# An earlier weight fold, another norm check and a new instruction order in a fused attention and gMLP kernel

## The chip, the cores and the metric

The kernel runs on one core of a Trainium2 chip. The metric is the device time of one execution in microseconds (us). The kernel before takes 265.9 us as the median of three runs (265.62 to 266.1).

An execution's profile has a span that is some 2 us shorter than its time. Stages below are read from the profiles. A ratio is the mean time of one kernel's fast runs over that of the other's in the same rounds, so it is not quite the ratio of the medians that are quoted.

## The reference

Two residual blocks over one sequence of 2,048 tokens with 448 features, both modulated by a condition vector `c`. The first is linear attention with 16 heads of 28 features and the feature map (softmax(p), softmax(-p)). The second is a gated MLP with a 2,048 by 2,048 spatial product.

```python
mod = (silu(c) @ w_mod).reshape(1, 6, 1, -1)          # sa, ca, ga, sb, cb, gb
h = layernorm(x) * (1 + ca) + sa
q, k, v = split_heads(h @ wqkv)
pq, pk = q @ w_phi, k @ w_phi                         # per head, 28 x 28
phi_q = concat(softmax(pq), softmax(-pq));  phi_k = concat(softmax(pk), softmax(-pk))
o = (phi_q @ (phi_k.T @ v)) / (phi_q @ sum(phi_k) + 1e-6)
x = x + ga * (o @ wo)
h = layernorm(x) * (1 + cb) + sb
z = gelu(h @ w_in);  z1, z2 = halves(z)
g = w_sp @ layernorm(z2) + b_sp                       # over tokens
x = x + gb * ((z1 * g) @ w_out)
```

## The kernel before

All weights that meet `h` are prepared on the chip. The per-head matrix `w_phi` is folded into the key weight (fold: transpose of the weight, `fold_T`, then a product with a block-diagonal copy of `w_phi`, called `BD`, `fold_pf`), its rows are scaled by 1 + ca, and the shift sa becomes one more row. The start-up in program order:

```python
    nc.scalar.dma_start(out=x_sb[:, 0:2, :], in_=xv[:, 0:2, :])             # x first on the ACT ring
    load_rows(nc.sync, wk_raw[:, :, 0:D], A_wqkv[:, D:2 * D])               # key weight, two loads
    nc.scalar.dma_start(out=wm1[:, :, D:960], in_=wmod_v[:, :, D:960])      # scale columns
    nc.sync.dma_start(out=phi[:], ...)                                      # w_phi
    nc.sync.dma_start(out=wm1[:, :, 0:D], in_=wmod_v[:, :, 0:D])            # shift columns
    # ... (cut)
    l1_rstd(0)                                                              # GpSimd
    l1_apply(0, nc.vector)
    nc.gpsimd.tensor_tensor(out=BD[:]..., in0=phi[:]..., in1=bmask[:]..., op=ALU.mult)
    # ... (cut)
    fold_T(wk_raw, wTk, False)
    cf = colform((1,))                                                      # 1 + ca as columns
    # ... (cut)
    own_turn(0)                                                             # first tile's transposes
    cf = colform((0,))                                                      # sa as columns
    # ... (cut)
    fold_sa(wk_raw, wTk)
    # ... (cut)
    for m in range(3):
        fold_pf(wTk, Wk, m, m % 2)
    fold_pf(wTk, Wk, 3, 1)
```

Everything behind the start-up is one long table of words. Each word is a step, and the order of the words is the program order on every engine; nothing else reorders them.

```python
    steps = dict(k=k_, e=e_, v=v_, ..., wsp=load_wsp, num=num_, t=t_, ad=ad_, oT=oT_, wo=wo_, h2T=hT_, z2=z2_, z1=z1_, zg=zg_, ...)
    for word in ORDER.split():
        name, *args = word.split(".")
        # ... (cut)
        steps[name](*map(int, args))
```

The words that the argument needs: `k`, `e`, `v`, `kv` are a tile's key product, exponentials, value product and key-value product, `kb1` copies their sum (the tile KVbd). Then `num` is the attention product of a tile, `t` its scaling on VectorE, `ad` an addition on GpSimd, `oT` a transpose by DMA, `wo` the output product (tile x_ps). `h2T` is the DMA transpose of the next normalised tile, `z2` and `z1` the two halves of the input product (both z_ps), `zg` the gelu of a z1 bank (it writes z1T). `wsp` loads and transposes a piece of the spatial weight, on the same queue as `oT` and `h2T`:

```python
    def load_wsp(tcn, u):
        q, hf = divmod(u, 2)
        r0 = tcn * TCHF + q * P
        nc.sync.dma_start_transpose(out=wsp_tiles[tcn][:, hf * 8:(hf + 1) * 8, q * P:(q + 1) * P],
                                    in_=B_w_sp[r0:r0 + P, hf * 1024:(hf + 1) * 1024])
    def oT_(i):
        oTs[i] = sm2.tile([P, KC, P], BF, name="oT", tag="oT", bufs=4)
        nc.sync.dma_start_transpose(out=oTs[i][:], in_=opad[i % NO][:])
    def zg_(st, fc):
        nc.scalar.activation(out=z1T[:, fc, st * 512:(st + 1) * 512], in_=ps.pop(("z1", st, fc)), func=ACT.Gelu_apprx_tanh, bias=b1[:, fc:fc + 1])
```

A check decides whether the fast path was allowed: a bound on the norm of the folded weights, made of 16 products (`gr`) and a square (`grc`). If it fails, a general path runs, which it doesn't for these inputs.

Of the kernel before, what the change touches and what calls it, by code (L numbers as in the profile page):

```python
# [8 lines left out]
ACT = mybir.ActivationFunctionType  # L9
# [6 lines left out]
P = 128  # L16
# [464 lines left out]
BY_ACT = (14, 15)  # L481
# [8 lines left out]
cc wv.1 k.0 bn.3 wv.0 wv.3 bv ag.3 wv.2 e.0.0 rp.1 bn.5 ld.7 k.1 bn.4 bvc ld.8 e.0.1 ag.5 ag.4 bn.6 gr.0 rp.2 e.1.1 ld1.2 rd.0 e.1.0 fq.1 grc.0 tm.2  # L490
v.1 to.2 fqc.3 la1.5 ld1.3 fqc.1 fq.0 bn.8 la1.4 vc.1 k.2 rc.0 fqc.0 bn.7 lT.4 tm.3 fqc.2 ag.8 v.0 e.2.0 to.3 ag.7 ag.6 v.2 mu.0 lT.5 rp.3 vc.0 rd.1
e.2.1 pq.1 v.3 vc.2 ld.3 bn.9 pqc.1 sq la1.7 rc.1 kv.0 vc.3 bn.10 pq.0 sqc la1.6 k.3 bn.11 pqc.0 ag.10 mu.1 lT.6 k.4 e.3.0 ag.9 rd.2 e.3.1 gt.0 rp.4
e.4.1 lT.7 pq.3 rd.3 e.4.0 k.5 pqc.3 ld.4 v.4 ca rc.2 gtc.0 ag.11 mu.2 e.5.0 v.5 e.5.1 wg.1 rc.3 vc.4 kv.1 rd.4 la1.9 pq.2 kv.2 vc.5 la1.8 lT.9 mu.3
k.6 pqc.2 rp.5 bn.12 sa.15 v.6 bn.13 lT.8 k.7 rd.5 vc.6 la1.10 v.7 e.6.0 ag.12 ag.13 rc.4 rp.6 e.7.1 rc.5 qp.0 lT.10 e.6.1 e.7.0 rd.6 sa.14 la1.11 q.4
mu.4 la1.12 lT.11 rd.7 cfb qe.4.0 la1.13 kv.3 rc.6 lT.12 cfc rp.7 k.8 qe.4.1 mu.6 vc.7 mu.5 k.10 e.8.1 ld.9 rc.7 kv.4 mu.7 la1.14 e.10.1 k.9 e.10.0
la1.15 lT.14 v.8 rd.10 e.9.1 e.8.0 kv.5 lT.13 e.9.0 k.11 rd.8 v.11 e.11.1 lT.15 rd.9 e.11.0 v.9 vc.8 rc.8 wsp.0.7 kv.6 qpe.0.1 rc.9 mu.8 k.12 rc.10
vc.9 kv.7 rd.11 ld.6 e.12.0 v.10 e.12.1 mu.9 vc.11 kv.8 ld.5 rc.11 vc.10 k.14 mu.10 k.13 rd.12 e.14.0 kv.9 mu.11 e.13.1 v.12 e.13.0 rc.12 kv.10 rd.13
vc.12 v.13 qpe.0.0 k.15 mu.12 e.14.1 rc.13 kv.11 vc.13 rd.14 v.14 e.15.0 kv.12 mu.13 vc.14 qp.1 rc.14 e.15.1 rd.15 kv.13 mu.14 v.15 rc.15 mu.15 kv.14
vc.15 wb.3 wg.0 qpe.1.1 wg.3 kv.15 zb qpe.1.0 kb1 wb.2 zbc kb2 wg.2 num.0 ws.0 num.1 sx.0 q.7 ws.3 sx.1 wbc.2 cr.0 q.6 cr.1 dn.0 dn.1 qe.7.0 ri.0 ri.1
w.0 w.1 wbc.3 q.5 t.0 qe.7.1 t.1 qe.5.1 ad.0 num.2 q.8 qe.6.0 ws.2 sx.2 ad.1 qe.6.1 oT.0 num.3 cr.2 ws.1 q.9 sx.3 qe.8.1 dn.2 oT.1 cr.3 ri.2 q.14 dn.3  # L500
qe.8.0 w.2 ri.3 t.2 qe.5.0 q.11 qe.14.1 w.3 ad.2 t.3 num.4 wo.0 sx.4 qe.14.0 oT.2 cr.4 ad.3 num.6 dn.4 qe.9.1 xc.0 q.15 qe.11.1 ri.4 ls.0 oT.3 qe.11.0
wo.1 w.4 la.0 t.4 qe.15.1 rs.0 q.13 sx.6 qe.15.0 xc.1 num.5 qe.9.0 cr.6 ap.0 q.10 ls.1 sx.5 qe.13.1 dn.6 ad.4 cr.5 la.1 h2T.0 q.12 dn.5 ri.6 ri.5
qe.10.1 w.5 w.6 rs.1 t.5 qe.10.0 wo.3 oT.4 qe.12.0 t.6 qe.12.1 num.8 ap.1 wo.2 sx.8 xc.3 qe.13.0 ad.5 h2T.1 z2.0 cr.8 xc.2 tb ad.6 dn.8 ls.2 oT.5 ri.8
gr.1 la.2 w.8 ls.3 ge.0 rs.2 oT.6 t.8 wo.4 num.7 ap.2 zs.0.0 z2.1 sx.7 la.3 zs.0.1 h2T.2 cr.7 za.0 dn.7 rs.3 ri.7 wo.5 w.7 wsp.0.1 ge.1 t.7 num.10
zs.1.0 ap.3 z2.2 xc.4 sx.10 ad.8 h2T.3 cr.10 zs.1.1 dn.10 ls.4 ad.7 wo.6 oT.8 ge.2 ri.10 la.4 w.10 za.1 t.10 rs.4 grc.1 num.9 oT.7 z1.0.4 xc.5 sx.9
xc.6 z2.3 ap.4 ls.5 cr.9 h2T.4 zs.2.0 ad.10 dn.9 z1.0.0 zs.2.1 ge.3 ri.9 wsp.0.2 la.5 w.9 wo.7 za.2 t.9 zn.0 rs.5 z2.4 oT.10 zs.3.0 zg.0.4 ls.6 ad.9
zs.3.1 num.12 wsp.0.0 ge.4 wo.8 xc.7 ap.5 za.3 la.6 sx.12 z1.0.5 ls.7 zn.1 rs.6 oT.9 cr.12 zs.4.0 num.11 zg.0.0 la.7 dn.12 z1.0.6 zs.4.1 h2T.5 sx.11
zg.0.5 ri.12 ap.6 cr.11 z1.0.3 w.12 zn.3 za.4 t.12 rs.7 h2T.6 wo.9 zn.2 dn.11 xc.8 z2.5 wsp.0.6 ri.11 xc.9 ap.7 w.11 ls.8 h2T.7 wo.10 t.11 ge.5 z1.0.2
zg.0.6 ad.11 zs.5.0 num.14 zs.5.1 z2.6 ad.12 oT.11 sx.14 cr.14 la.8 dn.14 za.5 ri.14 rs.8 w.14 xc.10 z1.0.1 ge.6 t.14 z1.1.3 zg.0.2 ap.8 zs.6.0 zg.0.3
num.13 ls.9 ad.14 z2.7 h2T.8 sx.13 zs.6.1 zn.4 cr.13 la.9 dn.13 za.6 oT.12 ri.13 wo.11 rs.9 w.13 ge.7 t.13 z1.1.0 zg.1.3 ls.10 num.15 ap.9 zs.7.0  # L510
zg.1.0 z2.8 la.10 ad.13 sx.15 zs.7.1 h2T.9 zn.6 za.7 xc.11 rs.10 wo.12 oT.13 ge.8 ls.11 z1.1.6 zg.0.1 oT.14 zs.8.0 ap.10 zn.5 z1.1.4 la.11 cr.15
zs.8.1 z2.9 h2T.10 dn.15 zg.1.6 za.8 ri.15 xc.12 rs.11 ls.12 wsp.0.3 z1.1.2 w.15 ge.9 t.15 ap.11 wo.14 zg.1.2 zs.9.0 h2T.11 ad.15 z1.1.5 zn.8 zs.9.1
wo.13 za.9 zn.7 oT.15 la.12 rs.12 z2.10 xc.13 xc.14 ap.12 ls.14 z1.1.1 ge.10 ls.13 z2.11 h2T.12 zg.1.1 zs.10.0 zg.1.4 la.13 zs.10.1 z1.2.1 za.10 ge.11
# [7 lines left out]
def fast_path(tc, A_x, A_wqkv, A_w_phi, A_wo, B_w_in, B_w_sp, B_b_sp, B_w_out, c, w_mod, out, flag):  # L521
# [781 lines left out]
```

## Time and profile before

| | kernel before |
|---|---|
| time, median of 3 | 265.9 us |
| span of the profile | 263.7 us |
| mean granted TensorE clock | 0.989 |
| first key product (k_ps) | 11.82 us |
| first exponential sum on VectorE | 15.39 us |
| key-value copy | 54.06 us |
| first spatial product (g_ps) | 139.40 us |

The page and the stages are read in the prediction below. Two more views matter for what came of it. The first is the timeline of TensorE between key-value copy and spatial product: start, duration, engine, line, operation, tiles written and read, shapes, count, and in brackets the idle time before it and what ended it.

```profile
86.01 0.93 PE L1087 MATMUL x_ps<-f_wo,oT 128*128 128x448 bf16 x4 [0.56 <-DVE w L1048]
...
93.31 0.93 PE L1087 MATMUL x_ps<-f_wo,oT 128*128 128x448 bf16 x4 [0.65 <-DMA oT<-f_opad]
...
120.03 1.69 PE L822 MATMUL z_ps<-f_win,h2T 128*128 128x448 bf16 x8 [0.31 <-DMA h2T<-f_xpad]
```

TensorE idles here for transposes that come late. (At 86.01 us the profile names a VectorE step, but the weight load of the same products had waited 1.06 us for oT.) The second view is the timeline of the SyncE queue that issues these transposes, with GpSimd's addition that makes the last tile, just ahead of the wait at 93.31 us.

```profile
85.46 1.31 SPq L996 DMA_TRANSPOSE f_wsp<-in_B_w_sp_dram  x1
87.31 1.19 SPq L1066 DMA_TRANSPOSE oT<-f_opad  x1
88.54 1.30 SPq L996 DMA_TRANSPOSE f_wsp<-in_B_w_sp_dram  x1
88.80 1.03 POOL L1062 TENSOR_TENSOR f_opad<-t 128x448 bf16<-128x448 bf16 x1
89.96 1.20 SPq L1066 DMA_TRANSPOSE oT<-f_opad  x1
```

Each transpose holds the queue for 1.2 to 1.3 us, one after the other. The token transpose at 89.96 us, for which TensorE waits at 93.31, stands directly behind a piece of the spatial weight (88.54 + 1.30 = 89.84) that is not needed before 139 us. In the queue that piece cost it next to nothing, though: GpSimd finished the tile only at 89.83 us. What came late was the landing, 3.31 us after the issue, where the median of these transposes is 2.5 us.

### The profile page before, as it was taken

Reading aid. Unit: us, or ns where it says so; the run is one execution under the profiler, and the core shown is the slowest. Engines: PE = TensorE matmul, PEld = TensorE weight load, DVE = VectorE, ACT = ScalarE, POOL = GpSimd, SP = SyncE. Lnnn points to the kernel's source line nnn. Section 1 sums busy time; section 2 is a strip of 40 time slices with the busy share of each in tenths; the row PEclk is TensorE's granted clock in tenths of the full one; section 3 lists DMA queues with packets and bytes.
Section 4 is the critical chain, followed back from the end, with each engine's and each line's share of the span. In section 5 each row is a group of like instructions: output and inputs, shape, how many; then the busy total and the mean of one; then the engine's idle time right before and its main releaser. Section 6 shows DMA issues by size and latency. Waiting matters only on the chain.

```text
span 263.7 us, 4389 instructions
## 1 busy us (share of the span) xinstructions
PE 250.0 (95%) x1564; PEld 129.6 (49%) x1584; DVE 163.7 (62%) x360; ACT 107.8 (41%) x212; POOL 90.3 (34%) x200
## 2 busy tenths in 40 slices
PE   6899999999999999999998999999999999999991
PEld 3766566665564545444443444444444444444440
DVE  4799999899999989875142454352433443342540
ACT  2799978578854758778895000000000000000000
POOL 5678970006776878757140190000000000000000
PEclk9799999999999999999999999999999999999998
DMA  7957976602456853442399999901000000001002
GB/s 196 307 151 142 199 108 118 223 0 42 80 85 105 125 110 62 87 94 40 66 212 184 243 157 207 194 18 37 17 0 17 20 20 15 0 20 35 19 20 62
DMA packets 69057, 25.29 MB, mean 96 GB/s; under 512 B 59105, under 2 KB 68898, under 8 KB 69026
## 3 DMA queue, kind: packets, MB, share of 16 engines
q1 hardware_dynamic: 68146, 24.18, 45.0%
q10 hardware_dynamic: 880, 0.75, 1.0%
q8 instruction: 14, 0.23, 0.4%
q14 instruction: 17, 0.14, 0.2%
HBM read 8.92 MB, written 1.84 MB: 41 GB/s over the span
## 4 chain that ended last, share of the span: by engine, by line
PE 73%; DVE 11%; DMA 6%; issue 3%; POOL 2%; ACT 1%; SPq 1%; DVEq 0%; POOLq 0%; ACTq 0%
PE g_ps L1195 37%; PE z_ps L822 8%; PE o_ps L1202 8%; PE k_ps L822 5%; PE v_ps L822 5%; DVE t L1056 4%; DMA h2T<-f_xpad 3%; PE kvacc L856 3%; DMA f_wm<-in_w_mod_dram 2%; DVE z2st L1110 2%; PE q_ps L822 2%; PE x_ps L1087 2%; DVE f_x L1091 1%; DMA oT<-f_opad 1%; POOL rs L1121 1%
## 5 line engine op out<-in xcount | busy, mean ns | idle before, releaser
L1195 PE MATMUL g_ps<-f_wsp,f_z2n 128*128 128x512 bf16 x327 | 73.7, 379 | 1.3 <-ACT f_z1T L1160 0.8
L1195 PEld LDWEIGHTS <-f_z2n 128*128 128x128 bf16 x448 | 43.8, 98 | 52.9 <-issue 1.1
L1197 DVE TENSOR_TENSOR gb<-g_ps,f_bsp 128x512 f32<-128x512 f32 x28 | 19.4, 692 | 67.9 <-PE g_ps L1195 67.9
L1247 ACT CAST ot<-o_ps 128x224 bf16<-128x224 f32 x1 | 0.3, 346 | 115.8 <-PE o_ps L1202 115.8
L822 PE MATMUL z_ps<-f_win,h2T 128*128 128x448 bf16 (+1 forms) x128 | 27.0, 352 | 0.5 <-DMA h2T<-f_xpad 0.5
L822 PE MATMUL z_ps<-h2T,f_win 128*128 128x512 bf16 (+1 forms) x107 | 26.6, 379 | 0.4
L1110 DVE BATCH_NORM_STATS2 z2st<-z2g 128x6 f32<-128x448 bf16 x32 | 19.2, 615 | 12.4 <-ACT z2g L1149 12.4
L1062 POOL TENSOR_TENSOR f_opad<-t 128x448 bf16<-128x448 bf16 x16 | 16.7, 1057 | 26.4 <-DVE t L1056 24.4
L1195 PE MATMUL g_ps<-f_hT,f_z2n 128*128 128x512 bf16 x110 | 24.9, 379 | 0.1
L1202 PE MATMUL o_ps<-f_wout,f_z1T 128*128 128x448 bf16 x112 | 23.5, 352 | 0.0
L1198 DVE TENSOR_TENSOR f_z1T<-gb,f_z1T 128x512 bf16<-128x512 f32 x28 | 20.7, 740 | 1.5 <-DVE gb L1197 0.5
L1149 ACT ACTIVATE z2g<-z_ps 128x896 bf16<-128x896 f32 x16 | 14.7, 919 | 14.5 <-PE z_ps L822 13.3
L1160 ACT ACTIVATE f_z1T<-z_ps,f_b 128x512 bf16<-128x512 f32 x28 | 18.2, 686 | 0.4 <-PE z_ps L822 0.4
L822 PEld LDWEIGHTS <-h2T 128*128 128x128 bf16 (+1 forms) x128 | 12.0, 97 | 12.2 <-DMA h2T<-f_xpad 1.3
L840 DVE TENSOR_REDUCE ksum<-f_E 128x32 f32<-128x896 bf16 x16 | 17.0, 1072 | 1.5 <-ACT f_E L829 1.4
L1153 ACT ACTIVATE f_z2n<-z2g,nm,rs 128x896 bf16<-128x896 bf16 x16 | 17.7, 1131 | 0.4 <-POOL nm L1124 0.3
L1056 DVE TENSOR_TENSOR t<-num,w 128x896 bf16<-128x896 f32 x16 | 17.2, 1087 | 0.4
L822 PEld LDWEIGHTS <-f_win 128*128 128x128 bf16 x112 | 10.7, 97 | 12.5 <-DMA h2T<-f_xpad 0.5
L829 ACT ACTIVATE f_E<-k_ps 128x448 bf16<-128x448 f32 x32 | 15.9, 549 | 1.8 <-PE k_ps L822 1.6
L1202 PEld LDWEIGHTS <-f_z1T 128*128 128x128 bf16 x112 | 11.0, 98 | 10.9
L822 PEld LDWEIGHTS <-f_hT 128*128 128x128 bf16 (+1 forms) x128 | 11.8, 98 | 8.8 <-issue 0.2
L1087 PE MATMUL x_ps<-f_wo,oT 128*128 128x448 bf16 x64 | 14.7, 352 | 1.2 <-DMA oT<-f_opad 0.6
(149 smaller groups left out, 340.2 us busy)
## 6 DMA issues: line engine op xcount, KB each, us to landing
out_dram<-ot SPq DMA_DIRECT2D x15, 112.0 KB, 1.7
f_x<-in_A_x_dram SPq DMA_DIRECT2D x3, 448.0 KB, 6.5
f_win<-in_B_w_in_dram SPq DMA_DIRECT2D x2, 672.0 KB, 7.2
f_wm<-in_w_mod_dram SPq DMA_DIRECT2D x1, 840.0 KB, 5.5
f_wout<-in_B_w_out_dram SPq DMA_DIRECT2D x1, 784.0 KB, 5.6
f_bsp<-in_B_b_sp_dram SPq DMA_DIRECT2D x1, 512.0 KB, 4.8
f_wm<-in_w_mod_dram ACTq DMA_DIRECT2D x1, 448.0 KB, 5.4
f_wm<-in_w_mod_dram SPq DMA_DIRECT2D x1, 392.0 KB, 5.5
```

What stands on the lines that cost most here:

```text
L822: nc.tensor.matmul(out, lhsT=lhs(kc, last[kc]), rhs=rhs(kc, last[kc]), start=(kc == 0), stop=(kc == KC - 1))
L840: nc.vector.tensor_reduce(out=cs["s", i][:], in_=Ering[i % NR][:].rearrange("p s (c f h) -> p (s c) h f", c=4, h=HP), axis=AX.X, op=ALU.add)
L1056: nc.vector.tensor_tensor(out=ts[i][:, 0:2 * D].rearrange("p (s h d) -> p s h d", s=2, h=H), in0=nv(i)[:, :, :, 0:DH], in1=cs.pop(("w", i) ...
L1062: nc.gpsimd.tensor_tensor(out=opad[i % NO][:, 0:D], in0=t[:, 0:D], in1=t[:, D:2 * D], op=ALU.add)
L1087: nc.tensor.matmul(ps["x", i][:, 0:D], lhsT=oT[:, cc, :], rhs=wo_s[:, cc, :], start=(i in RES_DVE and cc == 0), stop=(cc == KC - 1))
L1110: nc.vector.bn_stats(out=cs["z", i][:, hf, :], in_=z2gs[i][:, hf * D:(hf + 1) * D])
L1153: nc.scalar.activation(out=z2n[:, i, :], in_=z2gs.pop(i)[:], func=ACT.Identity, scale=rstd[:, 1:2], bias=nmr[:, 1:2])
L1160: nc.scalar.activation(out=z1T[:, fc, st * 512:(st + 1) * 512], in_=ps.pop(("z1", st, fc)), func=ACT.Gelu_apprx_tanh, bias=b1[:, fc:fc + 1])
L1195: nc.tensor.matmul(g[:], lhsT=z2n[:, s_, fc * P:(fc + 1) * P], rhs=wsp_tiles[tcn][:, s_, :], start=(s_ == 0), stop=(s_ == NT - 1))
L1197: nc.vector.tensor_tensor(out=gb[:], in0=g[:], in1=bsp[:, tsl], op=ALU.add)
L1198: nc.vector.tensor_tensor(out=z1T[:, fc, tsl], in0=gb[:], in1=z1T[:, fc, tsl], op=ALU.mult)
L1202: nc.tensor.matmul(o_ps, lhsT=z1T[:, fc, t * P:(t + 1) * P], rhs=wout_s[:, fc, :], start=(first and fc == 0), stop=(fc == FC - 1))
```

## The change

Its intent: fold the key weight before the shift is known, so that only the shift row is left when the shift columns land; start the scale columns and w_phi earlier; make the norm check cheaper on TensorE; move two tiles' statistics from ScalarE to VectorE; and lay a new order table over all of it. The diff, cut to its core:

```diff
-BY_ACT = (14, 15)
+BY_ACT = ()
 ORDER = """            (all words rearranged; two excerpts of the last lines)
-... z1.3.2 za.15 rs.18 zn.13 zg.3.3 zn.15 zg.3.0 zg.3.2 zg.3.4
+... zs.14.1 zg.3.4 ... zs.15.1 zg.3.3 zn.14 z1.3.0 za.15 rs.18 zg.3.2 zn.13 zn.15 zg.3.5 zg.3.0
 # loads
+    nc.scalar.dma_start(out=wk_raw[0:64, 3, 0:D], in_=A_wqkv[3 * P:D, D:2 * D])
+    nc.sync.dma_start(out=wk_raw[:, 0:3, 0:D], in_=A_wqkv[0:3 * P, D:2 * D]...)
     nc.scalar.dma_start(out=x_sb[:, 0:2, :], in_=xv[:, 0:2, :])
-    load_rows(nc.sync, wk_raw[:, :, 0:D], A_wqkv[:, D:2 * D])
     nc.scalar.dma_start(out=wm1[:, :, D:960], in_=wmod_v[:, :, D:960])
 # start-up
-    l1_rstd(0)
-    l1_apply(0, nc.vector)
     nc.gpsimd.tensor_tensor(out=BD[:]..., in0=phi[:]..., in1=bmask[:]..., op=ALU.mult)
+    l1_rstd(0)
     ...
+    l1_apply(0, nc.vector)
+    l1_apply(1, nc.vector)
+    keep_busy(2)
+    columns(cf_c, wmc, 128)                  # with fillers of 128 columns
     ...
+    turn_mm(0)
+    for m in range(3):
+        fold_pf(wTk, m)                      # unscaled, ahead of the shift
     ...
+    columns(cf_s, wms, 128)
     ...
+    fold_sa(wk_raw, sa_ps)
+    fold_pf(wTk, 3)
-    keep_busy(2, 256)
 # norm check
+    def gs_(which):
+        nc.scalar.activation(out=Wsq[:, 0:3, 0:D], in_=W[:, 0:3, 0:D], func=ACT.Square)
+        nc.scalar.activation(out=Wsq[0:65, 3, 0:D], in_=W[0:65, 3, 0:D], func=ACT.Square)
     def gr_(which):
-                nc.tensor.matmul(ps["gr", which][:, cc * CB:(cc + 1) * CB], lhsT=W[...], rhs=W[0:KB[kk], kk, cc * CB:(cc + 1) * CB], ...)
+                nc.tensor.matmul(ps["gr", which][:, cc:cc + 1], lhsT=Wsq[...], rhs=ones[0:KB[kk], :], ...)
```

## The prediction

> **What bounds the kernel now.** I read the page first: the granted clock is near full, TensorE is busy 95% of the span, and part 4 gives the chain that ended last 73% of TensorE.
>
> ```profile
> PE 250.0 (95%) x1564; PEld 129.6 (49%) x1584; DVE 163.7 (62%) x360; ACT 107.8 (41%) x212; POOL 90.3 (34%) x200
> ...
> PE 73%; DVE 11%; DMA 6%; issue 3%; POOL 2%; ACT 1%; SPq 1%; DVEq 0%; POOLq 0%; ACTq 0%
> ```
>
> So I looked for the 13.7 us in which TensorE is not busy, with the table of stretches (columns: stretch, length, then busy us and count for PE, PEld, DVE, ACT, POOL, then clock, DMA share, GB/s).
>
> ```profile
> 8.40:12.00 3.60, 3.56 (x56) 3.29 (x57) 2.54 (x6) 2.41 (x6) 2.90 (x20) 0.54 1.11 323
> 12.00:20.00 8.00, 8.00 (x75) 5.15 (x73) 8.00 (x23) 7.51 (x18) 5.40 (x12) 0.99 0.66 177
> 20.00:30.00 10.00, 10.00 (x94) 6.20 (x93) 10.00 (x20) 9.19 (x22) 8.52 (x17) 1.00 0.78 163
> ...
> 74.00:84.00 10.00, 9.46 (x77) 5.58 (x76) 9.83 (x27) 4.05 (x12) 7.92 (x16) 1.00 0.57 106
> 84.00:94.00 10.00, 8.74 (x55) 4.31 (x54) 9.67 (x30) 7.66 (x13) 7.28 (x15) 1.00 0.74 108
> ...
> 139.40:258.00 118.60, 117.85 (x551) 54.83 (x561) 48.48 (x73) 2.79 (x5) 7.87 (x7) 1.00 0.33 68
> ```
>
> Four stages. Start-up, to the first key product at 12.02 us. The key and value stage, to about 54 us, where TensorE, VectorE and ScalarE are all nearly full. The attention and gate stage, to 139.4 us, with TensorE idle about 4 us in all and VectorE nearly full. The spatial product, 118.6 us of TensorE, which the change leaves alone. Only the first 139.4 us can change.
>
> The chain in time order says what sets the start: the load of the modulation columns, then a run of TensorE work that ends in the key product.
>
> ```profile
> 2.86 5.53 DMA f_wm<-in_w_mod_dram
> 8.44 0.57 PE cf L771 x16
> 9.00 0.23 PE warm_ps L672
> 9.24 0.44 PE t_ps L728 x4
> 9.68 0.41 PE sa_ps L751 x16
> 10.08 1.52 PE pf L759 x16
> 11.60 0.43 PE warm_ps L672 x2
> 12.02 0.86 PE k_ps L822 x4
> ```
>
> The reader is to see that the 16 products of the fold (pf) took 1.52 us, 95 ns each, while the same products of the query fold later take 0.20 us for four, 50 ns each: the clock was 0.54 in this stretch. The timeline of VectorE shows the second clock of this stage, the first sum of the key softmax:
>
> ```profile
> 15.39 1.08 DVE L840 TENSOR_REDUCE ksum<-f_E 128x32 f32<-128x896 bf16 x1
> ...
> 54.06 1.09 DVE L1001 TENSOR_TENSOR f_KVbd<-kvacc,f_mask 112x896 bf16<-112x896 f32 x1 [0.65 <-PE kvacc L856]
> ```
>
> From there to the key-value copy VectorE has 38.7 us, of which some 2.3 us are idle: 36.4 us of work, hardly any slack.
>
> **What the Trainium skill says.** TensorE: Matmul & The Clock Gate, Part 1: the clock is halved after an idle window of about 3.4 us and restored after a busy one. The trace agrees: half clock from 8.7 to 12.1 us, 3.4 us. The same page, Engine queue depths, says that ScalarE and VectorE are strict FIFO; in the trace each runs in program order, so one long instruction at the head of ScalarE delays all behind it. DMA: Bandwidth & Descriptors, Queues, rings and completion order: each engine takes packets from the queues it has work for in turn, so a second ring gives order and not bandwidth. The trace has 318 to 342 GB/s from 2.5 to 5.5 us, and loads landed in the order of their issue, x at 3.4, key rows at 5.25, scale columns at 6.6, last key rows at 6.9, phi at 7.2, shift columns at 8.4.
>
> **The change part by part.**
>
> 1. *Fold ahead of the shift.* Three of four row blocks of the key weight are folded and scaled before the shift columns; only the shift row's block waits for them. Before: columns landed 8.39, k_ps over at 12.88, 4.5 us. What must follow the columns now: column products 0.57 plus three fillers (0.06 each at full clock) 0.75, copy 0.2, shift products 0.41, copy 0.2, four fold products 0.2, ScalarE scaling of 65 rows 0.65, last key product 0.2, hand-overs some 0.3 in all: 2.9 us. If nothing else were late this would win 1.6 us.
>
> 2. *But the layer norm gets later.* GpSimd now builds BD (0.93 us, waits for phi) ahead of the row statistics (5.53 to 7.17, 1.64 us). Phi is one issue earlier and has 57 KB of the key rows and the scale columns (459 KB) no longer in front; at some 335 GB/s plus the lag of 1.3 us that the loads of before show I get 5.6 to 5.9. The x tiles go from first to second on the ACT ring, behind key rows: about 4.6 to 5.3 in place of 3.4. BD is then over at 6.6 to 6.8, the statistics at 8.3 to 8.5, first normalised tile 8.7 to 8.9 (7.4 before). TensorE's order puts that tile's transposes ahead of the fold, so: transposes to 9.1, 12 fold products 0.6 at full clock to 9.8, shift columns to 10.5, shift products to 11.2, last block to 11.7, scaling to 12.3, k_ps over at 12.5. Win 0.4 us, not 1.6, and it needs full clock; at half clock it is a loss of some 0.4.
>
> 3. *Fillers.* Two products of 512 columns and three of 128, in gaps, so free; they are there for the clock. In the 3.4 us ahead of the drop the kernel of before streamed 20 transposes (2,560 columns); now up to 3,500. I take 60% that the clock stays.
>
> 4. *Norm check by column sums.* 16 products of 112 columns (0.80 us in the chain) become 16 of one column, which take 0.38 (row of the query shift): 0.42 us less on TensorE, twice, 0.8 us. Against it ScalarE squares the whole weight: 1,344 columns and 448. From 0.605 us for 448 (two in 1.21) and 1.08 for 896 (two in 2.16) the slope is 1.06 ns a column: 1.55 + 0.6 = 2.2 us each; the square of the sum falls from 0.56 to about 0.2. The first of these stands at the head of ScalarE before the value weights and the first exponentials, and TensorE's third item (gr) waits for it. From 12.3: squares to 14.5, TensorE, through with key and bias products at 13.3, idles 1.2 us; then value weights and bias 1.7, sum 0.35, four exponentials and a copy 2.1: VectorE's first sum at 18.7, not 15.4.
>
> 5. *Two tiles' statistics from ScalarE to VectorE.* ScalarE loses 2.8 us (27.9 to 29.25 and 31.4 to 32.85), VectorE gains two of 0.60 and two of 0.16, 1.5 us. In the new order VectorE does seven of the statistics while it waits for the exponentials, so its work after the first sum is nearly the same: 36.4 less a copy and an apply (0.8) plus half a microsecond of output-weight scaling, 36.1.
>
> 6. *Order table.* The key stage on VectorE: 18.7 + 36.1 = 54.8, the copy at 54.06 before: 0.7 us later, with a gap or two 1.0. TensorE needs about 40.7 us there plus its early idling, so it no longer sets the end. In return the next stage loses one VectorE scaling (0.4). At its end ScalarE gets two gelus ahead of the last normalisations, so that a PSUM bank is free when the spatial product wants it: up to 0.8 us, this wait of before.
>
> ```profile
> 139.40 1.89 PE L1195 MATMUL g_ps<-f_wsp,f_z2n 128*128 128x512 bf16 x7 [0.81 <-ACT f_z1T L1160]
> ```
>
> Sum on the path: +1.0 (key stage, start-up included) - 0.4 - 0.8 = -0.2 us. The 0.8 us of TensorE work in part 4 count only where TensorE is the bound; half of it, in the second check, may show: -0.4. That is 265.3; I say 265.2.
>
> **The rivals.**
>
> A. Start-up as meant: x lands with the key rows at 4.5, phi by 5.3, full clock throughout. Then k_ps is over near 11.8, VectorE starts about 0.7 earlier, and a better table wins 1 to 2 of the 4 us of idle in the attention stage: 262 to 263.5. For it: the table was remade for this start, and its end is visibly better. Against it: the bytes ahead of the shift columns are the same 1.5 MB.
>
> B. ScalarE becomes the bound: squares first, value weights and exponentials late, VectorE starved until ScalarE has caught up (its 2.8 us saving comes after 28 us). Half clock comes on top. Then the key stage ends 2 us or more later: 267 to 268.5. For it: ScalarE was busy 7.51 of 8.00 us from 12 to 20. Against it: VectorE has statistics to do meanwhile.
>
> C. All of it hidden: the attention stage waits for VectorE and for transposing loads whatever comes before, and the two meet again by 100 us: 265.5 to 266.3. For it: VectorE 9.83 of 10 us there.
>
> **Range and chances.** A 30%, the sum or C 50%, B 20%. 80% range 262.8 to 267.4. The line for faster by over 2% is 260.6, which needs more than all of A: 0.04. Slower by over 2%, 271.2: 0.02. Within: 0.94.
>
> **What would show it.** First normalised tile at 8.3 to 9 us; clock full from 8.7 to 12.1; k_ps over at 12 to 12.8; gr idle on TensorE of about 1 us for the squares; a squares instruction of 1.5 to 1.7 us; VectorE's first sum at 18 to 19.5; KVbd copy at 54 to 55.5; no wait over 0.3 us at the first spatial product; stretch after it unchanged within 0.3 us. If the first sum is late and the KVbd copy is not, I was wrong that VectorE bounds the key stage; if k_ps is over before 11.8, I was wrong on the loads; if the attention stage changes by over 2 us, the table did what I did not work out.

## The result

The changed kernel took 262.73 us (median of four runs, 262.06 to 262.95) against 265.92 us, a ratio of 0.9877 with a 95% interval of 0.9856 to 0.9898. That is within 2%, as predicted, but 2.5 us under the predicted 265.2 and just outside the range. Five more rounds of the same kernel later, beside other runs, gave 263.25 us (262.16 to 264.91) and 0.9935 (0.9898 to 0.9972). So the two occasions put the win at 3.3 and at 1.7 us; the more reliable question is where it arises.

The page of the kernel after, in its parts 1 and 4:

```profile
PE 249.1 (96%) x1570; PEld 129.5 (50%) x1590; DVE 163.6 (63%) x364; ACT 107.9 (41%) x208; POOL 90.3 (35%) x201
...
PE 84%; DMA 5%; DVE 3%; ACT 3%; issue 2%; POOL 1%; POOLq 0%; DVEq 0%
```

The chain that ended last has 84% of TensorE where it had 73%, and 3% of VectorE where it had 11%. By stage, the table of stretches of the kernel before (columns as in the prediction: stretch, length, busy us and count of PE, PEld, DVE, ACT, POOL, clock, DMA share, GB/s):

```profile
8.70:12.10 3.40, 3.40 (x52) 3.02 (x49) 2.33 (x6) 2.21 (x6) 2.60 (x20) 0.50 1.11 322
...
12.02:54.06 42.04, 41.93 (x399) 26.52 (x399) 39.60 (x81) 35.64 (x79) 21.84 (x41) 1.00 0.72 156
54.06:139.40 85.34, 81.43 (x520) 42.00 (x524) 68.53 (x184) 64.05 (x120) 52.59 (x102) 1.00 0.48 87
```

and of the kernel after:

```profile
8.70:12.10 3.40, 2.85 (x61) 2.54 (x62) 3.05 (x9) 1.55 (x4) 3.03 (x22) 1.00 1.12 305
...
11.91:54.48 42.57, 41.45 (x416) 26.07 (x416) 39.64 (x87) 35.73 (x73) 21.93 (x42) 1.00 0.66 157
54.48:136.57 82.09, 80.87 (x501) 42.19 (x507) 68.21 (x183) 63.70 (x121) 52.00 (x101) 1.00 0.49 84
136.57:255.09 118.52, 117.86 (x552) 54.81 (x561) 48.70 (x73) 3.95 (x7) 8.37 (x9) 1.00 0.36 72
```

The key stage ends 0.42 us later. The attention and gate stage is 85.34 - 82.09 = 3.25 us shorter. Of that, 2.69 us are idle time of TensorE (85.34 - 81.43 = 3.91 before, 82.09 - 80.87 = 1.22 after) and 0.56 us busy time; the split is rough, since both profiles lack some records of products (501 after, where e9, the same kernel again, has 508). The spatial product is unchanged, 118.5 us. The rest of the span after the last copy of output, 5.8 us before and 5.2 after, varies that much among the later profiles too and is not counted as a gain. VectorE might have bounded the attention stage, and the stage cut in two shows how far it does. First 40 us of it before, then after:

```profile
54.06:94.06 40.00, 37.63 (x290) 20.68 (x291) 39.26 (x110) 28.16 (x68) 26.22 (x45) 1.00 0.46 77
```

```profile
54.48:94.48 40.00, 39.05 (x281) 21.57 (x283) 39.25 (x108) 28.53 (x71) 26.28 (x44) 1.00 0.47 77
```

VectorE is full in both, with the same work. But TensorE gets 1.42 us more done in the kernel after while VectorE is full. In the rest of the stage VectorE is busy 29 us of 45.3 before and of 42.1 after, so it bounds nothing there; TensorE idles 1.54 us before and 0.27 after, and has less left to do.

The timeline after, where the prediction named instants:

```profile
5.30 0.63 DVE L702 BATCH_NORM_STATS2 l1st<-f_x 128x6 f32<-128x448 bf16 x1 [3.52 <-DMA f_x<-in_A_x_dram]
...
8.41 1.00 DVE L690 TENSOR_SCALAR f_xpad<-f_x,rstd,nmr 128x448 bf16<-128x448 bf16 x2
...
9.26 0.75 PE L755 MATMUL pf<-f_BD,f_wTk 112*128 112x112 bf16 x12
...
12.65 1.31 ACT L955 ACTIVATE f_Wsq<-f_Wk 128x1344 bf16<-128x1344 bf16 x1
...
18.34 1.08 DVE L850 TENSOR_REDUCE ksum<-f_E 128x32 f32<-128x896 bf16 x1
...
54.48 1.09 DVE L1019 TENSOR_TENSOR f_KVbd<-kvacc,f_mask 112x896 bf16<-112x896 f32 x1
```

The fold runs at full clock (12 products in 0.75 us), x lands 1.8 us later than before (5.28 against 3.46 us), VectorE's first sum is 2.95 us later than before and the copy only 0.42. And the timeline of TensorE in the attention stage, all waits over 0.15 us and the first spatial product:

```profile
65.74 0.58 PE L1045 MATMUL num<-f_KVbd,f_Eq 112*128 112x120 bf16 x8 [0.42 <-DVE t L1074]
...
81.73 1.69 PE L832 MATMUL z_ps<-f_win,h2T 128*128 128x448 bf16 x8 [0.24 <-DMA h2T<-f_xpad]
...
136.57 1.67 PE L1213 MATMUL g_ps<-f_wsp,f_z2n 128*128 128x512 bf16 x7
```

Of nine such waits before, two are left.

### The profile page after: what moved, and what is told of

Same layout as the page of the kernel before. It is cut to its first block, busy times and chain, and to the rows that moved or that the text cites. A ratio compares the mean times of both kernels' runs of the same rounds, so it can differ in the third digit from the quotient of the medians.

```text
span 260.3 us, 4412 instructions
## 1 busy us (share of the span) xinstructions
PE 249.1 (96%) x1570; PEld 129.5 (50%) x1590; DVE 163.6 (63%) x364; ACT 107.9 (41%) x208; POOL 90.3 (35%) x201
## 4 chain that ended last, share of the span: by engine, by line
PE 84%; DMA 5%; DVE 3%; ACT 3%; issue 2%; POOL 1%; POOLq 0%; DVEq 0%
PE g_ps L1213 37%; PE z_ps L832 16%; PE o_ps L1220 7%; PE v_ps L832 4%; PE k_ps L832 4%; PE x_ps L1105 3%; PE q_ps L832 3%; PE kvacc L866 3%; DMA h2T<-f_xpad 2%; PE num L1045 2%; PE warm_ps L673 1%; DVE t L1074 1%; DMA oT<-f_opad 1%; DMA out_dram<-ot 1%; PE tps L740 1%
## 5 line engine op out<-in xcount | busy, mean ns | idle before, releaser
L832 PE MATMUL z_ps<-h2T,f_win 128*128 128x512 bf16 (+1 forms) x107 | 26.0, 379 | 0.3
L832 PE MATMUL v_ps<-f_Wv,f_hT 128*128 128x448 bf16 x64 | 14.6, 352 | 0.4 <-ACT junk L968 0.4
```

The costliest lines, as they stand in the source:

```text
L832: nc.tensor.matmul(out, lhsT=lhs(kc, last[kc]), rhs=rhs(kc, last[kc]), start=(kc == 0), stop=(kc == KC - 1))
```

## The experiments

Eighteen runs were made. Stages are from each run's profile: start of the key products, key-value copy, length of the attention stage (copy to first spatial product). "Clock" says where the granted clock was under 1.00 in windows of the first 26 us.

| run | time us | ratio | key products | copy | stage | clock |
|---|---|---|---|---|---|---|
| before | 265.92 | 1 | 11.82 | 54.06 | 85.34 | half, 8.7-12.1 |
| after | 262.73 | 0.9877 | 11.91 | 54.48 | 82.09 | full |
| e1 old head, new tail | 263.37 | 0.9939 | 11.01 | 53.44 | 83.86 | full |
| e2 new head, old tail | 269.61 | 1.0161 | 12.54 | 55.11 | 88.28 | full |
| e3 before, loads moved | 267.73 | 1.0094 | 10.79 | 53.23 | 88.89 | full |
| e4 before, gelus early | 264.07 | 0.9951 | 12.68 | 55.03 | 84.80 | low, 8.7-15.5 |
| e5 no fillers | 264.67 | 0.9992 | 12.71 | 55.40 | 83.23 | low, 8.7-18.9 |
| e6 x first (one slow run of six left out) | 263.32 | 0.9923 | 13.68 | 56.28 | 82.30 | low, 12.1-18.9 |
| e7 squares late | 262.24 | 0.9896 | 12.13 | 54.00 | 82.10 | full |
| e8 old norm check | 263.25 | 0.9918 | 12.15 | 54.48 | 82.64 | full |
| e9 after again | 263.25 | 0.9935 | 12.01 | 54.57 | 82.40 | full |
| e10 before, loads in gaps | 264.41 | 0.9964 | 11.49 | 54.38 | 85.08 | low, 8.7-15.5 |
| e11 after, loads back | 264.53 | 0.9964 | 11.96 | 55.78 | 83.28 | low, 15.5-22.3 |
| e12 fold first, squares late | 261.90 | 0.9879 | 11.88 | 53.75 | 83.13 | full |
| e13 before, loads and gelus | 263.39 | 0.9948 | 10.72 | 53.15 | 83.92 | full |
| e14 after, gelus late | 264.32 | 0.9980 | 12.11 | 54.68 | 84.06 | full |
| e15 after, statistics on ScalarE | 262.89 | 0.9941 | 11.94 | 54.50 | 82.50 | full |
| e16 fold first only | 264.04 | 0.9968 | 11.97 | 55.79 | 82.43 | low, 15.5-22.3 |
| e17 old start, new rest | 263.43 | 0.9910 | 10.89 | 53.92 | 83.57 | low, 8.7-15.5 |
| e18 as e12 | 263.04 | 0.9902 | 11.97 | 53.84 | 82.59 | full |

The kernel before beside them took 265.09 us with e1 to e4, 265.49 with e5 to e8, 265.27 with e9 to e12, 264.71 with e13 to e16 and 265.91 with e17 and e18, so the ratios are the safer comparison. Nearly every ratio has an interval of plus or minus 0.003 to 0.005; stage lengths are free of the clock, which was full in the attention stage in all profiles but e3's. But each is one profile, and two profiles of one kernel differ by 0.31 us (after and e9) and by 0.54 (e12 and e18), so a difference of half a microsecond shows little by itself. From the first spatial product to the last copy of output every profile has the same length within 0.01 us.

The first question: is the gain in the order table of the attention stage, and in which part of it?

**e1, old head with new tail.** The kernel before, with only the table from the first `num` on taken from the changed kernel.

```diff
 # the kernel before
-ORDER = head_before + tail_before
+ORDER = head_before + ["wbc.3", "gr.1", "wbc.2", "ws.1"] + tail_after   # words not in the old kernel left out
```

> The kernel before, with only the attention and gate stage of its order table (from the first numerator on) taken from the changed kernel; start-up, key stage, norm check and code are those of before. Theory T (the gain is the new order of the attention stage: it has 2.7 us less TensorE idling there): KVbd copy at 54.1 +- 0.3 as before, stage from that copy to the first spatial product 85.3 -> 82 to 83 us, time 262.7 to 263.6. Rival R (the attention stage is shorter because of what the new start-up and key stage hand over to it): stage 84.5 or more, time 265.2 or more.

The stage went from 85.34 to 83.86 us: 1.48 of the 3.25 us with nothing else changed, between what the two theories said (82 to 83, and 84.5 or more). TensorE still waited 0.64 and 0.55 us for transposes of normalised tiles and 0.49 us on VectorE. In this kernel it has less query work to do meanwhile, since one query product (`q.4`) had been done before the stage; that this is the reason isn't shown.

**e2, new head with old tail.** The reverse.

```diff
 # the changed kernel
-ORDER = head_after + tail_after
+ORDER = head_after + tail_before        # with zbc and q.4, qe.4 put in behind num.0, num.1 and sx.1
```

> The changed kernel, with the attention stage of the order table of before (query products of the first stage moved into it, since the new key stage leaves one out). Theory T: stage from KVbd copy to the first spatial product 84.5 to 86 us, KVbd copy at 54.5, time 265.6 to 266.6, that is no gain or a small loss against before. Rival R: stage 82 to 83 us, time 262.5 to 263.5.

The stage took 88.28 us, nearly 3 us longer than the old table takes in its own kernel. It isn't a clean reverse: I had to insert a query product and its two exponentials near the head of the stage, and TensorE's largest waits there end with these exponentials on ScalarE (0.88 and 0.56 us); later it waits 0.85 us for a transposed tile and 1.06 us, at the first spatial product, for the bank of a gelu. No loss of this size was expected. What it suggests is that a table is tuned to what stands in front of it, not what the old table is worth.

**e3, loads moved, and e4, gelus early.** The kernel before with one feature of the new table each.

```diff
 # e3: the pieces of the spatial weight where the new table has them
-... oT.0 oT.1 ...            (wsp.0.1, .2, .0, .6, .3 among later transposes)
+... oT.0 wsp.0.1 wsp.0.2 oT.1 ... h2T.0 wsp.0.0 ...
 # e4: two gelus ahead of the last normalisations
-... zs.15.0 ... rs.18 zn.13 zg.3.3 zn.15 zg.3.0 zg.3.2 zg.3.4
+... zs.15.0 zg.3.4 ... rs.18 zg.3.3 zn.13 zn.15 zg.3.0 zg.3.2
```

> The kernel before, with only the transposing loads of the spatial weight moved: three to about 60 to 70 us and two to after the last normalised transpose, so that none stands among the transposes of attention output and normalised rows between 76 and 112 us. Theory T1 (two of the waits of TensorE there, 0.56 us at 86.0 and 0.65 us at 93.3, come from those loads on the same queue, which take 1.3 us each): both waits gone or under 0.2 us, time 0.8 to 1.4 us lower, 264.6 to 265.1. Rival (the waits come from VectorE, which feeds the transposes late): waits stay, time within 0.4 us of before.

> The kernel before, with two gelus of the gate put ahead of the last normalisations on ScalarE, so that two PSUM banks come free before the spatial product asks for one. As I said in the prediction, part 6: the 0.81 us wait of the first spatial product goes, time 0.6 to 0.9 us lower, 265.0 to 265.3. Rival (the normalised rows that the product needs come later in return, and it waits for them instead): a wait of 0.5 us or more on the normalisation within the first product, time unchanged within 0.3 us.

e3 was a miss: 0.9% slower, the stage 3.55 us longer. Its timelines of SyncE and TensorE:

```profile
60.38 2.65 SPq L996 DMA_TRANSPOSE f_wsp<-in_B_w_sp_dram  x2
...
67.66 0.93 PE L1087 MATMUL x_ps<-f_wo,oT 128*128 128x448 bf16 x4 [2.08 <-DMA oT<-f_opad]
```

Two pieces of the weight hold the queue for 2.65 us ahead of the second token transpose, and the old table wants that tile at once. TensorE waits 2.08 us, and in this profile its clock was 0.75 from 66.0 to 72.8 us, which costs another 6.8 x 0.25 = 1.7 us: the two make up the loss. In the new table the same place is nearly harmless: the output product of that tile comes a little over a microsecond later, at 68.8 us, just when the tile has landed (in e9 it waits 0.17 us there, in e12 0.61). So the loads do cost when they stand in the way, but where they are in the way depends on the rest of the table.

e4 removed the wait at the first spatial product entirely, and the stage became 0.54 us shorter, not 0.8. In its trace the wait of 0.56 us at 86 us has become two of 0.23 and 0.53 us (the second for a z1 gelu), and that of 0.65 us, for a transposed tile, is 0.70.

**e10, loads in gaps.** A gentler form of e3: three weight pieces go where the queue had nothing to do.

```diff
-... wsp.0.1 ... wsp.0.2 ... wsp.0.0 oT.9 ...
+... oT.9 ... oT.11 wsp.0.2 ... oT.15 wsp.0.0 ... h2T.15 wsp.0.1 ...
```

> The kernel before with three weight transposes (those at 77.4, 85.5 and 88.5 us) moved to places where the transposing queue had nothing to do, behind the transposes of tile 11, of tile 15 and of the last normalised tile. The attention stage was 85.34 us. Theory L (the weight transposes stand in front of the token transposes and make TensorE wait): the waits of 0.56 and 0.65 us at 86 and 93 us go, stage 84.0 to 84.4, ratio 0.995 to 0.997. Theory W (only the whole table balances the stage, a wait taken out comes back at the next shared point, as with the gelus): those waits shrink but others grow, stage 85.0 to 85.6, ratio 0.998 to 1.001.

The stage: 85.08, 0.26 us shorter. The wait at 93 us has gone, that at 86 halved, and a new one stands between, in the timeline of TensorE:

```profile
87.48 1.69 PE L822 MATMUL z_ps<-f_win,h2T 128*128 128x448 bf16 x8 [0.49 <-ACT f_z1T L1160]
```

By stage and waits this is the second theory's expectation: one wait taken out, another takes its place. The ratio of 0.9964 (0.9928 to 0.9999) would fit the first.

**e13, both edits.** The kernel before with the loads in gaps and the gelus early.

> The kernel before with both single edits: three weight transposes in gaps of the queue, and two gelus ahead of the last normalisations. Alone they made the attention stage 0.26 and 0.5 us shorter (85.34 to 85.08 and to 84.8). Theory M (waits stand in front of one another, an edit only shows where no other limit follows): both together win more than the sum, 1.2 us or more, stage 84.1 or less. Theory S (small independent wins): 0.7 to 0.8, stage 84.5 to 84.7. Either way short of the 82.1 of the changed kernel.

The stage: 83.92 us, 1.42 us shorter, where the two edits alone gave 0.26 and 0.54, in sum 0.80. That is the first theory's number (84.1 or less): the two seem to hide each other's win. It isn't shown, as the excess of 0.62 us is hardly more than the 0.54 between two profiles of one kernel, and in time e13 (0.9948) is no better than e4 alone (0.9951). Two moves in the table are thus worth as much in the old kernel as the whole new tail (1.48 in e1).

**e9, e11 and e14, the same two moves undone in the changed kernel.** e9 is the changed kernel unaltered, for the spread and as reference.

```diff
 # e11: three weight pieces back among the token transposes
-... oT.0 wsp.0.2 wsp.0.5 oT.1 ... h2T.0 wsp.0.3 ...
+... h2T.2 wsp.0.2 ... h2T.4 wsp.0.5 ... oT.10 wsp.0.3 ...
 # e14: two gelus behind the last normalisations
-... zg.3.4 za.14 ... zg.3.3 zn.14 ... zn.13 zn.15 zg.3.5 zg.3.0
+... za.14 ... zn.14 ... zn.13 zg.3.3 zn.15 zg.3.5 zg.3.0 zg.3.4
```

> The changed kernel unaltered, as the reference for the three beside it on the same chip, and to see its spread: ratio 0.985 to 0.990, attention stage (key-value copy to first spatial product) 81.8 to 82.6 us, TensorE idle in it 1.1 to 1.6 us.

> The changed kernel with three weight transposes put back among the token transposes at the places that they had in the kernel before (behind the normalised tiles 2 and 4 and the attention tile 10). Stage of the changed kernel 82.1 us. Theory L: waits of 0.5 us and more at the output products or at the gate products come back, stage 83.0 to 83.6. Theory W: output products there have 6 to 9 us of slack after their transposes landed (tiles 9 and 10), so nothing comes back: 81.9 to 82.4, and the early token transposes are freer.

> The changed kernel with two gelus of the last row put behind the last normalisations, as the kernel before had them. My record credited 0.8 us to this. If that holds here: a wait of 0.6 to 0.9 us at the first spatial product comes back and the stage grows from 82.1 or 82.4 to 83.0 or more. If ScalarE has slack at this end in the new order: under 0.3 us.

e9's stage: 82.40 us, as expected, but its ratio, 0.9935, is outside the 0.985 to 0.990 that I had given. e11's stage: 83.28, so 0.88 us come back, in one wait that its timelines of SyncE and TensorE show:

```profile
81.70 1.30 SPq L1014 DMA_TRANSPOSE f_wsp<-in_B_w_sp_dram  x1
...
86.67 0.93 PE L1105 MATMUL x_ps<-f_wo,oT 128*128 128x448 bf16 x4 [1.29 <-DMA oT<-f_opad]
```

That is the theory that the loads matter; the slack that I had read at tiles 9 and 10 did not protect another tile. e14's stage: 84.06, so 1.66 us come back, twice what I had credited, 1.35 of it in two waits of TensorE for banks that the gelus free:

```profile
137.15 1.03 PE L832 MATMUL z_ps<-h2T,f_win 128*128 128x512 bf16 x4 [0.78 <-ACT f_z1T L1178]
138.74 1.02 PE L1213 MATMUL g_ps<-f_wsp,f_z2n 128*128 128x512 bf16 x4 [0.57 <-ACT f_z1T L1178]
```

One reservation: the gelu that goes last here belongs to an earlier product of the new table's sequence than the one that stood last in the old table, so e14 is harsher than the kernel before was. 0.88 and 1.66 are 2.54 of the 3.25 us; some 0.7 us of the stage's gain I can't assign to one move. The sum is rough, since each number is one profile against e9's and the two need not add.

The second question: what did the start-up, the check and the statistics do?

**e5, no fillers.**

```diff
-    keep_busy(2)
-    columns(cf_c, wmc, 128)
+    columns(cf_c, wmc)
-    columns(cf_s, wms, 128)
+    columns(cf_s, wms)
```

> The changed kernel without the fillers: the two products of 512 columns and the six of 128 columns among the column products taken out. My part 3: they keep the clock full. If so, without them the clock falls to half for about 3.4 us in the start-up (products of the fold at 95 ns in place of 50), the key product ends 0.4 to 0.9 us later and the time is 0.2 to 0.8 us higher, 263.0 to 263.5. Rival (the new order alone keeps TensorE dense enough): clock full, time within 0.3 us of the changed kernel.

Without fillers the clock was 0.62 from 8.7 to 12.1 us and 0.50 from 12.1 to 15.5, the copy came at 55.40 (0.83 later than e9's), and the ratio was 0.9992 (0.9959 to 1.0026): by the means, the change's whole win is gone. By the medians, 264.67 against 265.49, a part is left; two of its six runs took over 266 us. The mean clocks of these runs are 0.978 to 0.990, those of e9's 0.988 to 1.000. The attention stage was 0.83 us longer than e9's too; why isn't shown. In all eleven profiles with the new start in its order of loads and with its fillers (after, e2, e7 to e9, e11, e12, e14 to e16, e18) the clock was full from 8.7 to 12.1 us. With the old start it was low in this stretch in four profiles (before, e4, e10, e17) and full in three (e1, e3, e13).

Part of this is chance: the traces' own records of the clock begin when it first became full, anywhere between 5.3 and 8.6 us (the seven products of 512 columns ahead of that take 3.0 to 3.2 us together, two of them behind it 0.59). With the old start it was halved next wherever that moment came by 7.03 us (the four) and not where it came from 7.13 us on (the three). With the new start and fillers it came by 7.00 us in six profiles (e11, e12, e14 to e16, e18), and the clock was halved next in none; in e5 it came at 6.08 us, and it was. So the comparison holds at like moments too, though for the fillers alone it rests on one profile and the six mean clocks.

**e6, x first on the ACT ring.** The load of x goes ahead of the last key rows again.

```diff
+    nc.scalar.dma_start(out=x_sb[:, 0:2, :], in_=xv[:, 0:2, :])
     nc.scalar.dma_start(out=wk_raw[0:64, 3, 0:D], in_=A_wqkv[3 * P:D, D:2 * D])
-    nc.scalar.dma_start(out=x_sb[:, 0:2, :], in_=xv[:, 0:2, :])
```

> The changed kernel with the first two x tiles first on the ScalarE ring again, the last key rows second. My part 2: the x tiles landed at 5.3 in place of 3.4 us and that, not the wait for phi, now dates the layer norm. If so: x lands at 3.4 to 4, row statistics on GpSimd start at 6.6 (then behind BD) in place of 7.0, first normalised tile 0.3 to 0.8 us earlier, key product over 0.3 to 0.8 earlier, time 0.2 to 0.8 us lower, 262.0 to 262.5. Rival (phi and BD take its place at once, or the last key rows come too late for the transposes of the fold): under 0.2 us either way.

A miss. x was there 1.8 us earlier (first statistics at 3.51 us), but the first tile was normalised 1.6 us later than in the changed kernel, as the timelines of GpSimd, VectorE and TensorE show:

```profile
7.54 0.93 POOL L788 TENSOR_TENSOR f_BD<-f_phi,f_bmask 112x448 bf16<-112x448 bf16 x1 [4.26 <-DVE f_wTk L742]
...
10.01 1.00 DVE L690 TENSOR_SCALAR f_xpad<-f_x,rstd,nmr 128x448 bf16<-128x448 bf16 x2 [2.11 <-POOL nmr L684]
...
10.51 0.40 PE L729 MATMUL t_ps<-f_ident,f_xpad 128*128 128x128 bf16 x4 [1.51 <-DVE f_xpad L690]
```

GpSimd's program has BD ahead of the row statistics, BD needs w_phi, and w_phi now landed 5.8 us after its issue in place of 3.9 (3.9 to 4.8 in all twelve other profiles with the new start). (The profile names VectorE as what ended GpSimd's wait, but that copy has nothing to do with BD, and w_phi's landing fits the time.) So the x load second on its ring and BD first on GpSimd are one decision. TensorE idled 1.51 us for the tile, and from 12.1 us on the clock was low. In the timed runs no loss shows: the ratio, 0.9923 (0.9891 to 0.9954), lies between the two of the changed kernel, and the profiled execution was the slowest of the five fast ones.

**e7, squares late, and e8, the old norm check.** e7 moves the squares of the key weight and their sums from the head of the key stage to its middle, near 36 us; e8 has the 112-column products of before and no squares.

```diff
 # e7
-cc gs.0 k.0 ... gr.0 ... grc.0 ...
+cc k.0 ... e.8.1 gs.0 ... e.9.1 gr.0 ... vc.8 grc.0 ...
```

> The changed kernel with the squares of the key weight, their column sums and the square of these moved from the head of the key stage to a gap of ScalarE at about 36 us (between exponentials of tiles 8 and 9). My part 4: at the head they hold up the value weights and first exponentials by 1.8 us and TensorE by about 1 us. If VectorE bounds the key stage, as I said: first key sum 1.5 to 2 us earlier, KVbd copy 1 to 1.8 us earlier, time 1 to 1.8 us lower, 260.9 to 261.7. Rival (the stage is bound by TensorE or by waits that take the delay in): first key sum earlier, KVbd copy within 0.5 us, time within 0.5 us.

> The changed kernel with the norm check of before (16 products of 112 columns of the weight with itself, no squares on ScalarE), all else as changed. My part 4: without squares the first exponentials come 1.8 us earlier, TensorE pays 0.4 us twice. If VectorE bounds the key stage: KVbd copy 0.6 to 1.6 us earlier, attention stage 0 to 0.2 longer, time 0.4 to 1.5 us lower, 261.2 to 262.3: the cheaper check on TensorE is then a loss. Rival (TensorE bounds it): time 0.4 to 0.8 us higher.

With the squares late the copy comes at 54.00 us, 0.5 us earlier than in the changed kernel (54.48 and 54.57). That is the rival's number, not the 1 to 1.8 us that a bound by VectorE would give: the first sum came 1.0 us earlier, at 17.33 us. With the old check the copy comes at 54.48, no different, and the attention stage is 0.2 to 0.6 us longer. Against e9, TensorE has 0.25 us more work from the first key product to the copy (41.81 against 41.56), but idles 0.52 us in place of 1.00. So the cheaper check loses by idling at the head what it saves in work; the place of the squares was the flaw. The ratios (0.9896, 0.9918, and 0.9935 for e9, each plus or minus 0.003 to 0.004) don't tell the three apart.

**e15, statistics on ScalarE again.** `bn.14` and `bn.15` become `sa.14` and `sa.15`, with `BY_ACT = (14, 15)`.

> The changed kernel with the statistics of the tiles 14 and 15 on ScalarE again (two times 1.35 us), at the places of the new order, and 1.5 us less on VectorE. If VectorE bounds the key stage in the new order (40.2 busy of 43.0 us): key-value copy 0.5 to 1.5 us earlier. If TensorE or ScalarE's exponentials bound it: unchanged within 0.3 or later by up to 1.5 us. My record said the move was neutral on the path.

Copy at 54.50, stage 82.50, ratio 0.9941: as e9 within the spread. The move is neutral in time, and it tells which engine bounds the key stage. The table of stretches from the first sum to the copy, of e9 and then of e15:

```profile
18.44:54.57 36.13, 36.13 (x358) 22.98 (x356) 34.36 (x69) 29.57 (x60) 17.25 (x31) 1.00 0.70 143
```

```profile
18.37:54.50 36.13, 36.13 (x358) 22.97 (x356) 33.35 (x64) 31.88 (x68) 17.44 (x31) 1.00 0.68 143
```

VectorE has 1.0 us less work and ScalarE 2.3 us more, and the stretch is as long as before: TensorE is busy in all of it.

**e12, e16 and e18, a version that combines what won.** e16 has the three early fold products ahead of the first tile's transposes (with one filler less, and the second tile normalised a little later); e12 has that and e7's late squares; e18 is e12 again.

```diff
-    l1_apply(1, nc.vector)
     # ... (cut)
-    turn_mm(0)
-    turn_out(0, hT[:, :, 0:P], True)
-    keep_busy(1, 256)
+    l1_apply(1, nc.vector)
     # ... (cut)
     for m in range(3):
         fold_pf(wTk, m)
+    turn_mm(0)
+    turn_out(0, hT[:, :, 0:P], True)
```

> The changed kernel with two edits meant to win: the three early fold products go ahead of the first tile's transposes (in the changed kernel TensorE waited 0.47 us for that tile with the fold ready), and the squares of the key weight and their sums go to the middle of the key stage. From the run with squares late alone, whose key-value copy came 0.5 us earlier, and 0.25 to 0.4 us of the first: key-value copy 53.5 to 54.0, ratio to the kernel before 0.983 to 0.987, 0.5 to 0.9 us under the changed kernel run beside it. If VectorE's chain is full from the first sum on, only the squares count and it is 0.5; if the attention stage is limited by its own chain of VectorE and transposes, half of it is lost there.

> The changed kernel with only the fold ahead of the first tile's transposes, the squares where the change has them. Start of the key products 0.1 to 0.4 us earlier than 11.9 to 12.0, first exponential sum 0.1 to 0.4 earlier than 18.4. If the key stage carries that through: copy at 54.1 to 54.4 and 0.2 to 0.4 us in all; the best version's 1.3 us would then be mostly the squares' place.

> The version with the fold first and the squares late once more, on the same chip as the run with the old start-up: ratio 0.985 to 0.991, key-value copy 53.6 to 54.0, full clock from 12 to 22 us.

e12 took 261.90 us where e9 took 263.25 on the same chip; its ratio, 0.9879, just misses the 0.983 to 0.987 expected. The means of their six runs are 262.10 and 263.41, a difference of 1.3 us with a 95% interval of 0.2 to 2.4 us worked out from their scatter. e18 has 0.9902 on another occasion, so that it beats the changed kernel is likely but rests on one pair of runs. e16 alone shows little: its key products were no earlier and its copy came at 55.79, because its clock fell in the key stage. e11's did too; the table of stretches of e11:

```profile
15.50:18.90 3.40, 2.96 (x36) 2.25 (x35) 2.06 (x9) 3.23 (x10) 3.03 (x7) 0.75 0.44 120
18.90:22.30 3.40, 3.40 (x24) 2.30 (x23) 2.75 (x6) 2.82 (x6) 2.48 (x5) 0.75 0.43 87
```

Two windows at 0.75 are one stretch of some 3.4 us at half clock, and the copy came at 55.78, 1.2 us late. The idling of TensorE behind the early squares (5.80 us busy of 6.80 from 12.1 to 18.9 us in the changed kernel, 6.30 in e18) goes ahead of it. It happened in two of seven profiles with the squares at the head (after, e2, e9, e11, e14 to e16) and in none of three with them late (e7, e12, e18). That the early squares risk a drop of the clock is suggested by this, not shown.

**e17, old start with everything else new.** The start-up of before, with the new table, check (squares late) and statistics behind it.

> The kernel before's start-up (its loads, fold, x first) with the new order table, column-sum check and statistics on VectorE behind it, and the squares in the middle of the key stage. Theory K (the change's start-up is the slower one at full clock): key products from 10.7 to 11.0 us at full clock, or 11.8 at half clock; key-value copy 52.7 to 53.3 or 53.8 to 54.3; attention stage 82.0 to 83.0; ratio 0.981 to 0.986. Theory N (the new table is tuned to the late start, ScalarE and VectorE can't use the early one): key-value copy 53.7 or later at full clock too, ratio 0.987 to 0.990 as the best version so far.

The key products began at 10.89 us, 1.1 us earlier than e18's, but in this profile the clock was low just then:

```profile
8.70:12.10 3.40, 3.29 (x46) 2.31 (x43) 2.89 (x8) 2.31 (x5) 2.63 (x21) 0.76 1.11 321
12.10:15.50 3.40, 3.25 (x27) 1.64 (x26) 3.40 (x13) 1.39 (x3) 2.69 (x6) 0.74 1.10 320
```

The copy came at 53.92 and the ratio was 0.9910 against e18's 0.9902. The two start-ups are worth the same within what these runs resolve. Neither theory's stage and ratio fit: the stage, 83.57 us, was 1.0 longer than e18's, which isn't explained.

## Why the prediction was right or wrong

**The step that failed is part 6, the order table.** It let the attention stage gain 0.4 us for a scaling that moved and "up to 0.8 us" for the gelus, and 0.4 us more were taken for the second norm check: at most 1.6 us. The stage gained 3.25. It was mis-sized in two ways. The gelus were priced by the one wait that they would remove (0.81 us); with the rest of the new table around them they are worth up to 1.66 (e14). And the pieces of the spatial weight that stand among the token transposes were not priced at all, though their queue was there to be read; they are worth 0.88 in the new table (e11). Alone in the old kernel the two are worth only 0.54 and 0.26 (e4, e10), together 1.42 (e13). So adding up single waits of the old trace, as the sum did, seems to understate a table that removes several at once.

**Part 6 on the key stage** was right in number by luck. It gave VectorE 36.1 us of work from the first sum to the copy and said that TensorE no longer sets the end. The copy did come 36.14 us after the first sum, but it was TensorE that was busy in 36.03 of them, VectorE in 34.38. The stretch is as long (36.13 us) in e2, e5, e6, e9, e14 and e15, whenever the first sum came, and e15 took work off VectorE without making it shorter. The trace of before had it to be read: TensorE busy in 38.56 of the 38.67 us, VectorE in 36.23. TensorE's need was mis-sized: 40.7 us plus idling were said, and from the first key product to the copy it had 41.45 us of work and 1.12 idle.

**Rival A** had the number, 262 to 263.5, and half of the mechanism: a better table wins 1 to 2 us of idle time in the attention stage (2.69 came). Its start-up did not happen (k_ps over near 11.8 us said, 13.14 measured).

**Rival C**, which shared 50% with the sum, drew a wrong conclusion from a right reading. VectorE is full in the first 40 us of the stage, before and after. But over the stage it is busy 68.5 of 85.3 us, while TensorE has 81 us of work: what counts is that TensorE always has something to do that needs nothing from VectorE just then, and in the first 40 us the new table gives it 1.42 us more of that.

**Parts 1 and 2, the start.** Right in mechanism: x at 5.3 us (4.6 to 5.3 said), the first normalised tile done at some 8.9 (8.7 to 8.9 said; TensorE takes it up at 8.91). That the fold ahead of the shift wins nothing because the layer norm became late fits this, but putting the fold first (e16) didn't bring the key products forward either. The size was off: k_ps was over at 13.14 us (its four products start at 11.91 and last 1.23), not at 12.5, so the win of 0.4 us over the 12.88 of before was a loss of 0.26. The last block's products, said to be over at 11.7, started at 11.69 and ended at 12.08, so the scaling began at 12.11. (The 1.5 MB of rival A count the shift columns themselves.)

**Part 3, fillers.** The clock stayed, as given 60%; it did so in eleven of eleven profiles, so 60% was too low. The fillers of 128 columns are six, not three. That the trace agrees with the page on the clock holds for the 3.4 us alone: no idle window went ahead, as TensorE was busy for 2.19 us of the 3.40 from 5.3 to 8.7 and its longest gap was 0.74. Their worth was in the sum only as a condition; e5 has it at 0.8 us of the copy, and at more in the ratio.

**Part 4, squares.** The squares took 1.31 + 0.56 = 1.87 us, not 2.2. The first sum at 18.34 us (18.7 said) is near, but not by the squares alone: with them gone from the head (e7) it still came at 17.33, so they cost it 1.0 us. The copy at 54.48 (54.8 said, with gaps 55.1) is near by the luck told above. The +1.0 us for the key stage measured +0.42 in the profiled pair, but the kernel before had its clock halved for 3.4 us there; against the profiles with the old start at full clock (copy at 53.15 to 53.44, e13, e3 and e1) the change costs 1.0 to 1.3 us.

**Part 5, statistics.** Neutral as said (e15), but because TensorE bounds the key stage, not because VectorE has time for them at its head.

**Spatial product.** Unchanged within 0.01 us, as said, and no wait over 0.3 us at its first product, as said.

In sum: the +1.0 came as +0.42, the profiled before having lost the clock; the -1.6 came as -3.25; the span's end gave -0.6 that is spread. My own marker, an attention stage that changes by over 2 us, is what happened. What stays open is some 0.7 us of the stage, and how large the change's win is over many chips, with 0.9877 and 0.9935 measured.

## What to carry to other kernels

When an order table is replaced, list every idle gap of the bounding engine in the stage, and for each ask which queue entry or bank holds it, a non-urgent one above all: a table that moves them together can gain more than the gaps one by one. An engine that is full in half of a stage is not the bound of the stage: ask whether the engine with the most work over the whole stage can run ahead meanwhile, and take work off the supposed bound in one run, as e15 did. And look at the clock of the profile of before, window by window, before a start-up is compared with it.

## What the Trainium skill lacked or had wrong

- TensorE: Matmul & The Clock Gate, Part 1: it says that the window is free-running, so that the same kernel meets it differently from run to run. The runs agree: the old start was at half clock near 8.7 to 15.5 us in four of seven profiles. It has the clock halved after an idle window of about 3.4 us; here no such window went ahead of any of the nine falls that the profiles show before a kernel's end, the longest gap of TensorE in the 3.4 us before one being 0.3 to 2.1 us. The page gives nothing on holding the clock with fillers; here two of 512 columns and six of 128, in gaps, went with a full clock in eleven of eleven profiles, and without them it was 0.62 and 0.50 (e5).
- DMA: Bandwidth & Descriptors, DMA Transpose (X-bar): it says that two transposing streams in flight at once can corrupt each other, which is a reason for having all transposes on one queue. Neither it nor another page says how long one of these sizes holds its issuing queue; here 1.2 us for a token tile and 1.3 us for a piece of the spatial weight, one after the other, and in the median 2.5 and 4.0 us from issue to landing.
- DMA: Bandwidth & Descriptors, Queues, rings and completion order: packets of both rings taken in turn don't tell a reader the landing order. Putting 224 KB of x ahead of 56 KB on one ring moved the landing of a 24.5 KB load on the other ring from 3.9 to 5.8 us after its issue (e6).
